# Cutting the token and result transfers of a planned S4-and-MLP kernel in two pieces instead of four, with a newly searched order

## The chip, the cores and the metric

The kernel runs on one core of a Trainium2 chip. The metric is the device time of one execution in microseconds; for the kernel before it is the median of three runs.

## The reference

A token mixer with an S4 convolution and an MLP gate, on 2048 tokens of 512 channels, all float32. Cut to what matters:

```python
xn = layernorm(x)                                  # x = A_u, [1, 2048, 512]
# S4: K[d, l] = Re sum_n C exp(dt A l) dt B, then a long convolution by FFT
y = irfft(rfft(pad(xn)) * rfft(pad(K)))[:L] + xn * Dskip
# MLP on the same xn: two shifted token mixings, then a channel MLP
h = gelu(layernorm(xn) @ w1)
x1 = xn + concat(shift(+1), shift(-1), shift(+2), shift(-2) of h's quarters) @ w2
b = x1 + gelu(layernorm(x1) @ w3) @ w4             # 512 -> 1376 -> 512
return x + y * silu(b)
```

## The kernel before, in words

The tokens lie in one SBUF tile `X` of 128 partitions, 16 slices `s` and 512 channels. Token 64 t + 16 r + s is in partition 32 i + t of slice s, where r is `ORDER[i]` and `ORDER` is 0, 2, 1, 3. A piece of 32 partitions therefore holds one r, and its rows lie 64 tokens apart in memory; within a row the slices are contiguous.

All work is first recorded as operations (matmul, activation, DMA and so on) with what they read and write, by the class `Plan`; nothing is written out in the order in which it runs. `order()` then simulates the engines with a cost for each operation and takes, on each engine, the ready operation with the smallest number in the table `DUE`. The table `PIN` says for each operation that VectorE (DVE) or ScalarE (ACT) could do which of the two does it. Where the simulation sees TensorE (PE) waiting for longer than `LEAST` microseconds it puts idle products (`pick.fill` matmuls of an identity into a spare bank) in front of the waiting matmul. `issue()` writes out ACT's table loads (L496), the idle products (L498) and all operations (L499), so nearly every row of the trace has line 499, and the tile names tell the steps apart. Each engine runs its own list in order. DMAs are issued from SP's list, the result's stores (`E.store`, L630) from SP's or ACT's.

The steps by their tile names:

- `loads()` (L832) brings the S4 parameters (`rawA`, `rawC`), the weights (`w`, `wst`), constants (`ks`, `ev`, `is`), `Dt` (the skip weights, four DMAs of 2 x 64 numbers) and the tokens `X`. The tokens come through `by_r` (L808) for slices 0-1, 2-3, 4-7, 8-11 and 12-15, four DMAs of 32 partitions each time.
- DVE takes `stats` of X slice by slice for the layer norm; DVE or ACT normalise X in place.
- From about 20 to 370 us DVE and ACT build the convolution kernel's phases and magnitudes (`pt`, `mag`), while TensorE transforms the tokens (`uin`, `ue`, `scr_Ud`, `scr_Uh`) and the kernel (`kin`, `k1e`), through scratch tensors in memory.
- The MLP's products `pb<-x1T,w3h` (up) and `pa<-w4h,ghl` (down) fill TensorE's time between the transforms.
- `products` multiplies the spectra (`pr`), `inverse` (L1195) loads `zin` and transforms back, and X is multiplied by the gate in place.
- `finish(g)` (L1215) loads the raw tokens again into `xr`, through `by_r` for four slices at a time, adds them, and stores the result with four DMAs of 32 partitions for each piece of a group.

All DMAs share 8 semaphore lanes in turn; a DMA on a lane waits until the last one on that lane has landed.

Of the kernel before, what the change touches and what calls it, by code (L numbers as in the profile page):

```python
# [24 lines left out]
S = 16  # L25
# [71 lines left out]
class Op:  # L97
# [20 lines left out]
SPAN, LEFT, LEAST = 0.224, 0.3, 0.8  # L118
# [517 lines left out]
def kernel(  # L636
# [579 lines left out]
    xr = {}  # L1216
# [363 lines left out]
```

## Time and profile before

| what | value |
|---|---|
| median of 3 runs | 535.5 us (535.47 to 535.63) |
| the profiled execution | 537.38 us, its span 535.6 us |
| PE, DVE, ACT busy | 511.1, 450.9, 400.8 us |
| bytes moved by the DMA engines | 109.44 MB, mean 204 GB/s |
| granted TensorE clock, mean | 0.99 |

Times inside the execution count from the start of the span. A row of the timeline or of the chain gives start, duration, engine, line, operation, output and inputs, and the number of instructions merged in it. "SPq" and "ACTq" are DMA issues on those engines' queues. A row of a group gives busy time, mean ns of one instruction, and the idle time before it with what ended it. A row of a window gives its length, each engine's busy time with its instructions, the granted clock, the mean busy share of the 16 DMA engines and the rate in GB/s; the share can exceed 1 where packets overlap. A row of a tile gives the shortest, median and longest instruction in ns, with the first and the last start in us. A row of waits gives the sum, the number and the longest.

### The profile page before, as it was taken

How to read it: one execution, taken by the hardware profiler on the slowest of the kernel's cores; microseconds unless marked ns; L12 is line 12 of the kernel's file. 1: busy time of each engine (PE TensorE's matmuls, PEld its weight loads, DVE VectorE, ACT ScalarE, POOL GpSimd, SP SyncE). 2: the span in 40 equal slices, each digit the busy share in tenths (PEclk: the TensorE clock that was granted, in tenths of full speed). 3: DMA queues.
4: the chain of work that ended last, by engine and by line, in shares of the span. 5: the costliest groups of instructions: out<-in, count | busy, mean ns of one | idle time of the engine just before them, and what ended most of it. 6: DMA issues, size and time to landing. Idle time of an engine off the chain costs nothing.

```text
span 535.6 us, 14336 instructions
## 1 busy us (share of the span) xinstructions
PE 511.1 (95%) x6055; PEld 333.1 (62%) x6055; DVE 450.9 (84%) x783; ACT 400.8 (75%) x597; POOL 0.7 (0%) x6
## 2 busy tenths in 40 slices
PE   8789999999999999999999999999999999999992
PEld 8776666774343666565676676666655666566650
DVE  6899999999999999999999999999553267754593
ACT  4999999999998999998989999885336315322420
POOL 0000000000000000000000000000000000000000
PEclk9899999999999999999999999999999999999997
DMA  7994689983886506456333643547989859979986
GB/s 192 258 222 160 227 249 254 281 233 121 296 269 221 101 7 163 140 194 178 112 129 70 180 158 107 118 164 207 251 332 320 282 175 286 258 234 275 310 252 186
DMA packets 95329, 109.44 MB, mean 204 GB/s; under 512 B 40289, under 2 KB 74337, under 8 KB 94369
## 3 DMA queue, kind: packets, MB, share of 16 engines
q1 hardware_dynamic: 94592, 106.95, 69.4%
q10 hardware_dynamic: 672, 1.57, 1.0%
q8 instruction: 47, 0.77, 0.6%
q14 instruction: 18, 0.14, 0.1%
HBM read 64.46 MB, written 37.75 MB: 191 GB/s over the span
## 4 chain that ended last, share of the span: by engine, by line
PE 68%; DVE 10%; ACT 10%; DMA 7%; issue 2%; SPq 2%; ACTq 0%; DVEq 0%
PE pb L499 22%; PE pa L499 22%; PE pd L499 13%; PE pc L499 11%; DVE pt L499 7%; DMA X<-in_A_u_dram 4%; ACT pt L499 3%; SPq L499 2%; ACT ue L499 2%; DVE X L499 1%; ACT L496 1%; DMA scr_Ud<-ue 1%; ACT wst L499 1%; DMA cst<-c_gp 1%; DMA rawC<-in_A_B_re_dram 1%
## 5 line engine op out<-in xcount | busy, mean ns | idle before, releaser
L499 PE MATMUL pb<-x1T,w3h 128*128 128x256 f16 (+1 forms) x1056 | 124.9, 273 | 0.0
L499 PE MATMUL pa<-w4h,ghl 128*128 128x512 f16 (+1 forms) x528 | 123.4, 380 | 0.0
L499 PEld LDWEIGHTS <-w3h 128*128 128x128 f16 (+1 forms) x1056 | 102.6, 100 | 28.8 <-issue 11.6
L499 PEld LDWEIGHTS <-ghl 128*128 128x128 f16 (+1 forms) x528 | 49.4, 98 | 60.6 <-issue 9.2
L499 ACT ACTIVATE g<-pb,wsc 128x512 f32<-128x512 f32 (+1 forms) x48 | 30.7, 650 | 47.6 <-PE pb L499 43.6
L499 ACT ACTIVATE pt<-pt 128x2048 f32<-128x2048 int32 x32 | 61.0, 1908 | 2.4 <-DVE pt L499 2.3
L496 ACT ACT_TABLE_LOAD x48 | 61.6, 1283 | 1.6 <-PEq L1568 0.7
L499 DVE TENSOR_TENSOR pt<-mag,pt 128x1024 f32<-128x1024 f32 x48 | 58.1, 1215 | 0.1
L499 PE MATMUL pd<-w,hT 128*128 128x512 f32 x116 | 53.3, 600 | 2.4 <-DVE X L499 1.9
L499 DVE SCALAR_TENSOR_TENSOR ghl<-g,wsc,ghl 128x512 f16<-128x512 f32 (+1 forms) x48 | 33.5, 700 | 11.6 <-ACT ghl L499 11.3
L499 ACT ACTIVATE mag<-par 128x128 f32<-128x128 f32 x160 | 41.1, 463 | 0.1
L499 ACT ACTIVATE ghl<-g,wsc 128x512 f16<-128x512 f32 (+1 forms) x35 | 24.0, 688 | 20.5 <-PE pa L499 19.0
L499 PEld LDWEIGHTS pd<-w,hT 128*128 128x128 f32 x116 | 21.1, 190 | 27.7 <-issue 23.3
L499 DVE TENSOR_TENSOR pt<-pt 128x2048 f32<-128x2048 f32 x16 | 36.4, 2281 | 0.9 <-ACT pt L499 0.9
L499 PEld LDWEIGHTS pc<-pt 128*32 128x32 f32 x2048 | 29.5, 110 | 8.4 <-issue 5.8
L499 PE MATMUL pc<-pt 128*32 128x64 f32 x2048 | 32.4, 220 | 1.9 <-DVE pt L499 1.0
L499 ACT ACTIVATE pt<-pt,halfpi 128x2048 f32<-128x2048 f32 x16 | 32.0, 1999 | 0.1
L499 PE MATMUL pb<-xT,w 128*128 128x256 f32 x128 | 29.6, 383 | 1.4 <-ACT xT L499 1.4
L499 DVE TENSOR_TENSOR pr<-pd,uin 128x1024 f32<-128x1024 f32 x16 | 19.3, 1219 | 11.5 <-PE pd L499 11.5
L499 PEld LDWEIGHTS pb<-xT,w 128*128 128x128 f32 x128 | 23.6, 190 | 7.8 <-ACT xT L499 3.3
L499 DVE TENSOR_TENSOR pr<-pd,kh 128x1024 f32<-128x1024 f32 x16 | 19.3, 1218 | 6.7 <-PE pd L499 6.0
L499 PE MATMUL pb<-xT,w1h 128*128 128x256 f16 x192 | 22.5, 273 | 0.0
(160 smaller groups left out, 787.8 us busy)
## 6 DMA issues: line engine op xcount, KB each, us to landing
wst<-in_B_w_dram SPq DMA_DIRECT2D x20, 512.0 KB, 5.1
scr_Ud<-ue SPq DMA_DIRECT2D x16, 512.0 KB, 3.9
uin<-scr_Ud SPq DMA_DIRECT2D x32, 256.0 KB, 4.3
cst<-c_gp SPq DMA_DIRECT2D x16, 384.0 KB, 4.0
scr_Uh<-uh SPq DMA_DIRECT2D x8, 512.0 KB, 3.2
scr_Kfa<-k1e SPq DMA_DIRECT2D x8, 512.0 KB, 3.7
kin<-scr_Kfa SPq DMA_DIRECT2D x16, 256.0 KB, 4.1
scr_Zda<-z1e SPq DMA_DIRECT2D x8, 512.0 KB, 5.0
```

The lines of the kernel that those rows point to most:

```text
L496: self.engines["ACT"].preload_act_table_set(SETS[table])
L499: ins = [getattr(self.engines[op.eng], name)(*args, **kw).ins for name, args, kw in op.calls]
```

## The change

- Tokens and result are viewed as `(t b a s) d -> a b t s d`, with a and b of size 2. `by_r` loops over the two a, and each DMA has 64 partitions in SBUF (b and t together) and b of 2 by t of 32 rows in memory. The placement of the tokens in X is the same.
- All stores go through `by_r`, on SP alone. X takes 10 DMAs instead of 20, xr 8 instead of 16, the result 18 instead of 36.
- A wait is filled with idle products for 0.87 of its length (`FILLED`) instead of all of it.
- There are 1796 operations instead of 1832, and `DUE` and `PIN` hold newly searched numbers.

```diff
-SPAN, LEFT, LEAST = 0.224, 0.3, 0.8
+SPAN, LEFT, LEAST, FILLED = 0.224, 0.3, 0.8, 0.87
...
 PIN = (
-    "10111111111111111111111111111111111111111111111110101101101111111100111110010011101111111111101110100000111111"
...
+    "10111111111111111111111111111111111111101001011011111111001111100100111011111111101011101111001111111111100111"
...
-                    pick.fill = max(0, int((t - start - LEFT) / SPAN))
+                    pick.fill = max(0, int((t - start - LEFT) * FILLED / SPAN))
...
-    xv = u[0].rearrange("(t r s) d -> r t s d", r=4, s=S)
-    ov = out[0].rearrange("(t r s) d -> r t s d", r=4, s=S)
+    xv = u[0].rearrange("(t b a s) d -> a b t s d", a=2, b=2, s=S)
+    ov = out[0].rearrange("(t b a s) d -> a b t s d", a=2, b=2, s=S)
...
     def by_r(sb, dr, to_dram=False):
-        for r in range(4):
-            a, d = sb[32 * r : 32 * r + 32], dr[ORDER[r]]
-            Q.dma_start(d, a) if to_dram else Q.dma_start(a, d)
+        for a in range(2):
+            part = sb[64 * a : 64 * a + 64]
+            Q.dma_start(dr[a], part) if to_dram else Q.dma_start(part, dr[a])
...
-        by_r(X[:, 0:2], xv[:, :, 0:2])
+        by_r(X[:, 0:2], xv[:, :, :, 0:2])
...
-            by_r(X[:, s0:s1], xv[:, :, s0:s1])
+            by_r(X[:, s0:s1], xv[:, :, :, s0:s1])
...
-            by_r(xr[q], xv[:, :, 4 * q : 4 * q + 4])
+            by_r(xr[q], xv[:, :, :, 4 * q : 4 * q + 4])
...
-            for r in range(4):
-                E.store(ov[ORDER[r]][:, x], X[32 * r : 32 * r + 32, x])
+            by_r(X[:, x], ov[:, :, :, x], True)
```

SP's list at the start, where the parameters and the first tokens are loaded (shapes are those of the transfer's output side; xN merges equal rows). Before:

```order
L499 DMA rawC<-in_A_C_im_dram 128x2x128
L499 DMA X<-in_A_u_dram 32x1024 x7
L499 DMA ks_81<-c_ks 128x128
L499 DMA X<-in_A_u_dram 32x1024
L499 DMA rawC<-in_A_B_re_dram 128x2x128
L499 DMA wst<-in_B_w_dram 128x4x256
L499 DMA rawC<-in_A_C_re_dram 128x2x128
L499 DMA ev<-c_ev 128x44
L499 DMA rawC<-in_A_B_im_dram 128x2x128
L499 DMA X<-in_A_u_dram 32x2048 x5
```

The same place in the list of the changed kernel:

```order
L497 DMA X<-in_A_u_dram 64x1x1024 x2
L497 DMA rawC<-in_A_C_re_dram 128x2x128
L497 DMA X<-in_A_u_dram 64x1x1024
L497 DMA ev<-c_ev 128x44
L497 DMA X<-in_A_u_dram 64x1x1024
L497 DMA rawC<-in_A_B_re_dram 128x2x128
L497 DMA rawC<-in_A_C_im_dram 128x2x128
L497 DMA X<-in_A_u_dram 64x1x2048
```

Eight pieces of the first four slices became four pieces of 64 partitions; parameters and weights stand between pieces of X as before, `ks` and `wst` later.

SP's list at the end, from the last reloads `xr` to the last store. Before:

```order
L499 DMA xr<-in_A_u_dram 32x2048
L499 DMA zin<-scr_Zdb 128x4x256
L499 DMA xr<-in_A_u_dram 32x2048
L499 DMA zin<-scr_Zdb 128x4x256 x2
L499 DMA zin<-scr_Zda 128x4x256
L499 DMA out_dram<-X 32x1024 x17
L499 DMA out_dram<-X 32x512
L499 DMA out_dram<-X 32x1024
L499 DMA out_dram<-X 32x512 x3
```

The end of SP's list in the changed kernel:

```order
L497 DMA xr<-in_A_u_dram 64x1x2048
L497 DMA scr_Zdb<-z1e 128x1024
L497 DMA xr<-in_A_u_dram 64x1x2048 x5
L497 DMA scr_Zdb<-z1e 128x1024
L497 DMA zin<-scr_Zda 128x4x256 x2
L497 DMA zin<-scr_Zdb 128x4x256 x8
L497 DMA zin<-scr_Zda 128x4x256
L497 DMA out_dram<-X 2x32x1024 x14
L497 DMA out_dram<-X 2x32x512 x4
```

The reloads now stand together in front of eleven loads of `zin`, and all 18 stores follow one another on SP, two for each piece of a group.

ACT's list at its end, with its share of the stores and the gate's last activations (`X<-X`). Before:

```order
L499 ACTIVATE ghl<-g_485,wsc 128x512
L499 ACTIVATE ghl<-g_487,wsc 96x256
L496 ACT_TABLE_LOAD
L499 ACTIVATE warm<-g_487 96x1
L499 DMA out_dram<-X 32x1024 x5
L499 ACTIVATE X<-X 128x512 x2
L499 DMA out_dram<-X 32x1024
L499 DMA out_dram<-X 32x512
L499 DMA out_dram<-X 32x1024
L499 DMA out_dram<-X 32x512 x3
```

The end of ACT's list in the changed kernel:

```order
L497 ACTIVATE ghl<-g_485,wsc 128x512
L497 ACTIVATE g_487<-pb_100,wsc 96x256
L494 ACT_TABLE_LOAD
L497 ACTIVATE warm<-g_487 96x1
L497 ACTIVATE ghl<-g_487,wsc 96x256
L497 ACTIVATE X<-X 128x512 x2
```

No store is left in ACT's list, and the last table load stands ahead of the last `ghl` instead of behind it.

More of the change, by code (lines that the diff above doesn't have):

```diff
@@ L226 @@
 PIN = (
-    "10111111111111111111111111111111111111111111111110101101101111111100111110010011101111111111101110100000111111"
-    "11111001111100100111011111111111110111111111111111111111111111101011011010101111111111111111111111111111111111"
-    "01110110110101011111111111111111111111101111111011011010111111101101101010111111111111111111111111111101111111"
-    "11111111111111111011010111111111110110101111111111111111111111111111110011111110110101010110111101101010111111"
-    "11111111010101010101010101010101111111111111111111111101101111111111111111111111111111111111111111111111111101"
@@ L232 @@
-    "11111111111111111111111111101101111111111111111111111111111111111111111011011111111111111111111101101111101111"
-    "10111110111110111110111110111110111110111110100110011010000000001111110001111111101111111000111111111111111100"
-    "01111111101111111000111111110101000000000111111000111111110111111100011111111011111110001111111101111111000111"
-    "11111011101111110111111001110111001111001111100111101111110011111001111100111001100111100111110011110111111111"
-    "01111001111100111001111111101111110111111101111110111111101111110111111101111110111111101111110111111101111110"
@@ L237 @@
-    "11111110111111011111110111111010100000000011111100011111111011111110001111111101111111000111111110111111100011"
-    "11111111010000000001111110001111111111111111000111111110111111100011111111011111110001111111101110011111001111"
-    "10111110111111110111111001111001111100111110011111001110011001111001111100111100111110011111001111101111011101"
-    "11110111111001111001111100111110111111011110111101111011111100111101111110011111001111100111111100111100111110"
-    "01111001111100111110011111011111100111110011110011011111111011110011100111011111111111110111111111110111111111"
@@ L242 @@
-    "11111111111111011111111111011111111111011111111111111111111111010000000001111111111111111111111111111111111111"
-    "111111111111111100111111011111111110110111111101101011111111001100111100"
+    "10111111111111111111111111111111111111101001011011111111001111100100111011111111101011101111001111111111100111"
+    "11001001110111111111010111111111111111111111111111111010110110101011111111111111111111111111111111110111011011"
+    "01011111111111111111111111111101001110110110101011111011011010101111111111111111111111111011100111111111111111"
@@ new lines @@
+    "11111110110101111111111101101010111111111111111111111111111101110111101101010101101111011010101111111111111101"
+    "01010101010101010101011111111111111111111111011011111111111111111111111111111111111111111111111111011111111111"
+    "11111111111111111011011111111111111111111111111111111111111110110111111111111111111111011011011111111011111011"
+    "11101111101111101111101111101111101001100110100000000011111100011111111011111110001111111111111111000111111110"
+    "11111110001111111101010000000001111110001111111101111111000111111110111111100011111111011111110001111111101110"
@@ new lines @@
+    "11111101111110111100110011110011111001111001111100111110011111001110011001111001111101111101111111110111100111"
+    "11001110011111111011111101111111011111101111111011111101111111011111101111111011111101111111011111101111111011"
+    "11110111111101111110101000000000111111000111111110111111100011111111011111110001111111101111111000111111110101"
+    "00000000011111100011111111011111110001111111101111111000111111111111111100011111111011100111110111111011110011"
+    "10111101111110111110111111011111100111110011101110011110011111001111011111100111110011111011110011011111001111"
@@ L244 @@
+    "10111110011111011111100111110011101111111110011111001111011111100111110011111011111011011111001111100111101111"
+    "11001111101111110111111001111100111100110111111110111101111101111011111111111101111111111111111111111101111111"
+    "11110111111111110111111111110111111111111111111111111100000000011111111111111111111111111111111111111111111111"
+    "111111111111111111111111111111111111"
 )
```

180 rows, old and new, of the table DUE are left out of this document.

## The prediction

> **What bounds the kernel now.** I read the page first: the engines' shares, the queue that carries the data, and the chain of waits.
>
> ```profile
> PE 511.1 (95%) x6055; PEld 333.1 (62%) x6055; DVE 450.9 (84%) x783; ACT 400.8 (75%) x597; POOL 0.7 (0%) x6
> DVE  6899999999999999999999999999553267754593
> q1 hardware_dynamic: 94592, 106.95, 69.4%
> PE 68%; DVE 10%; ACT 10%; DMA 7%; issue 2%; SPq 2%; ACTq 0%; DVEq 0%
> ```
>
> TensorE is busy for 511.1 of 535.6 us, and the chain lies on it for 68%. A change that leaves TensorE's work alone can win only in the rest: the start, a few holes, the end. The queue's line holds a second fact. Its 106.95 MB took 69.4% of 16 engines' 535.6 us, so an engine moved 106.95 MB / (0.694 x 16 x 535.6 us) = 18.0 GB/s while busy. Next I asked for the two ends, in the chain in order of time and in the timeline of SP, ACT and DVE.
>
> ```profile
> 14.20 9.11 DMA X<-in_A_u_dram
> 23.32 10.98 DMA X<-in_A_u_dram
> 517.53 6.60 PE pa L499 x30
> 526.32 1.30 DVE X L499 x2
> ...
> 511.49 21.83 SPq L499 DMA_DIRECT2D out_dram<-X  x22
> 525.60 4.20 ACTq L499 DMA_DIRECT2D out_dram<-X  x6
> 527.65 0.69 DVE L499 TENSOR_TENSOR X<-X,xr 128x512 f32<-128x512 f32 x1
> SPq L499 <- DMA out_dram<-X: 9.9, 5, 5.4
> ```
>
> At the head the chain runs for 20 us over loads of X. At the tail TensorE stops at 524.13, the last residual add at 527.65 + 0.69 = 528.34, and SP issues stores until 511.49 + 21.83 = 533.32: the span ends 7.3 us after the last add. SP spends 9.9 us of that stretch on other stores' landings, 5.4 at once. What the change touches are thus X's loads, the reloads xr, and the stores, and how long each takes sets both ends.
>
> **The change part by part.** First the bytes, from the page's list of transfers:
>
> ```profile
> X<-in_A_u_dram SPq DMA_DIRECT2D x12, 256.0 KB, 8.5
> X<-in_A_u_dram SPq DMA_DIRECT2D x8, 128.0 KB, 3.9
> xr<-in_A_u_dram SPq DMA_DIRECT2D x16, 256.0 KB, 5.3
> out_dram<-X SPq DMA_DIRECT2D x18, 128.0 KB, 2.1
> out_dram<-X ACTq DMA_DIRECT2D x10, 128.0 KB, 3.2
> out_dram<-X ACTq DMA_DIRECT2D x4, 64.0 KB, 2.0
> out_dram<-X SPq DMA_DIRECT2D x4, 64.0 KB, 1.7
> ```
>
> X is 4.19 MB, xr 4.19 and the result 4.19. All three are recut by one edit, and not only in number: a piece was 32 rows against 32 rows. Now its SBUF side is 64 partitions, and its memory side is `b` = 2 outermost, then `t` = 32. The two sides share only one outermost cut, the one in halves. If a transfer is dealt to the engines by its outermost dimension, as I take it to be, a piece of 32 went to 16 engines and a piece of 2 x 32 goes to 2.
>
> The nearest rows to such a pattern are Dt's loads, the only ones before with 2 outermost:
>
> ```profile
> L499 SPq DMA_DIRECT2D Dt<-in_A_Dskip_dram x4: 579/593/770, 21.0 to 35.4; - x4
> L499 SPq DMA_DIRECT2D X<-in_A_u_dram x20: 311/419/472, 5.9 to 34.3; - x20
> L499 DVE BATCH_NORM_STATS2 stats<-X x16: 658/682/694, 11.9 to 49.7; 128x6 f32<-128x512 f32 x16
> L499 SPq DMA_DIRECT2D xr<-in_A_u_dram x16: 310/420/1523, 372.4 to 501.8; - x16
> 372.39 2.85 SPq L499 DMA_DIRECT2D xr<-in_A_u_dram  x4
> 478.93 1.74 SPq L499 DMA_DIRECT2D xr<-in_A_u_dram  x4
> 509.55 0.36 SPq L499 DMA_DIRECT2D zin<-scr_Zda  x1
> DMA to landing us min/median/max: 3.0/6.9/11.0
> ```
>
> (The last of these lines is for the loads of X.) They show the price on SP: 0.59 us an issue against 0.42 (X, 20 issues to 10, so 8.4 us of SP's time to 5.9; nobody waits for that difference). They don't show engines: Dt's 0.5 KB prints no landing time. In the trace's semaphore records, which no view prints, each of them has fewer updates than a piece of X; that speaks for the dealing, on a transfer too small to have a price.
>
> The Trainium skill, "DMA: Bandwidth & Descriptors", section on why a DMA increments its semaphore by 16, states such a rule: the number of engines is the largest one up to 16 that divides the slowest dimension of size over 1 on both sides, and the hardware queues take the lowest-numbered engines. By it all three transfers go over engines 0 and 1, as in my sum; without it, evenly spread, the sum is rival B's. No run so far shows it for a large transfer.
>
> What two engines are worth is in the windows:
>
> ```profile
> 0.00:12.00 12.00, 10.65 (x73) 10.65 (x74) 7.74 (x24) 5.31 (x14) 0.70 (x6) 1.00 0.75 191
> 12.00:40.00 28.00, 22.71 (x153) 20.05 (x151) 26.09 (x100) 27.46 (x73) 0.00 (x0) 0.94 1.05 239
> 390.00:395.00 5.00, 5.00 (x48) 2.97 (x34) 3.95 (x5) 1.23 (x2) 0.00 (x0) 1.00 1.02 413
> 480.00:490.00 10.00, 10.00 (x118) 7.03 (x116) 5.51 (x8) 2.68 (x4) 0.00 (x0) 1.00 1.00 264
> 490.00:500.00 10.00, 10.00 (x92) 6.05 (x91) 3.89 (x6) 6.44 (x7) 0.00 (x0) 1.00 1.01 299
> 500.00:512.00 12.00, 12.00 (x186) 7.08 (x185) 7.42 (x11) 2.10 (x3) 0.00 (x0) 1.00 1.09 298
> ```
>
> An engine in full use moved 413 / (16 x 1.02) = 25.3 GB/s at best, and 239 / (16 x 1.05) = 14.2 at worst, when sixteen competed. Two that run nearly alone compete with little, so I take 25.3; 18.0 and 14.2 stay for the range.
>
> *Head.* 191 x 12 + 239 x 28 = 9.0 MB move in the first 40 us, of which 4.8 are not X. Engine 0 now carries 4.8/16 = 0.30 and X's half, 2.10: 2.40 MB, 95 us at 25.3. From about 2 us on, X is complete at 97; before, DVE's last statistics of X ran at 49.7 to 50.4. DVE executes in order, and the page has it at 9 tenths or more from its third slice (27 us) on, so little can be made up: +47 us (+85 at 18.0, +121 at 14.2). Transfers issued behind X wait too, since each has a sixteenth of its bytes on those engines; within these 47 us they are counted already.
>
> *Reload at 372 us.* xr's first quarter, 1.05 MB, occupies the two engines for 0.52 / 25.3 = 21 us, in front of spectra that TensorE reads soon after. Between nothing and 21: 10.
>
> *Tail.* Three quarters of xr (1.57 MB an engine) are issued from about 479 on, as before. The last three windows carry 9.2 MB from 480 to 512, less 3.15 of xr 6.1, a sixteenth 0.38. Then 2.10 of stores: 1.95 / 25.3 = 77 us, 2.10 / 25.3 = 83 us, and some 5 between them until the first result is ready (0 to 10). 479 + 77 + 5 + 83 = 644, and with 47 and 10 the span ends at 701. Nothing hides this: TensorE's remaining work after 479 is 45 us.
>
> *Stores on SP alone.* 36 issues on two queues become 18 on one. The 5.4 us hole (a store on SP waits for one of ACT's queue, which stands behind the last silu) goes. Spread over 16 engines, the end would be the last add, 528.34, two issues of 0.6, and a landing of 2.1: 531.6 against 535.6, **-4.0**. On two engines nothing of that is seen, since the drain decides.
>
> *Idle products and the new order.*
>
> ```profile
> L496 ACT ACT_TABLE_LOAD x48 | 61.6, 1283 | 1.6 <-PEq L1568 0.7
> 79.24 1.60 PE L498 MATMUL pd<-ident 128*128 128x128 f32 x12
> 111.44 0.83 PE L498 MATMUL pa<-ident 128*128 128x128 f32 x6
> 465.39 5.70 DMA cst<-c_gp
> ```
>
> The order has 4 table loads less (at most 4 x 1.283 = 5.1 us, on an engine that waits elsewhere), and 51 idle products for 57, none of them past the first 40 us; the two late groups, 1.60 and 0.83, stand in waits that stay. The chain's wait for cst may go. I put these at **-2** together, between -5.1 and +2.4 (if the two late groups' waits prove longer in the new order). In the two-engine case this drowns.
>
> **The sum.** The profiled execution took 537.38 us, its span 535.6, 1.8 around it; the median of the runs, 535.5, is 1.9 less. Forecast: 701 + 1.8 - 1.9 - 2 + 2 for the last landing, **701 us**. Its own range: if only half of the head's delay passes on, and neither 10 nor 5 is paid, 479 + 77 + 83 + 24 = 663, and 660 with the order's gain; a little faster engine leads to 650. At 18.0 GB/s: 479 + 108 + 117 + 5 + 85 + 15 = 809, which I think too slow for engines that compete with little, so 790.
>
> **The rivals.**
>
> *B, faster: the transfers still go over 16 engines*, because the queue cuts them by rows or bytes and not by the outermost dimension. For it: every large transfer of before runs that way, and the windows with a share above 1.00 show all sixteen filled. Against it: none of those has 2 outermost, and Dt's records. Then SP's queue at the end decides: 537.38 - 4.0 - 2 - 1.9 = **529.5**, between 526 and 534 (-5.1 and +2.4 in the place of -2). Chance 0.14.
>
> *C: one side alone decides.* If only the side read counts, X and xr go over 2 engines and the stores over 16: 479 + 77 + 47 + 10 = 613, then the last 15 us of TensorE's work from its last zin load (509) to 524 and the 7.5 of the end: 636. If the side written counts, only the stores do: first store 511.5 before, 83 us of drain: 595, less what the order gains. **585 to 645**, chance 0.06.
>
> **How the numbers follow.** A (two engines) has 0.80: the pattern allows nothing else if dealing goes by the outermost dimension, and the one row of this kind has records that fit. A's own range, 650 to 790, holds it 19 times in 20, 0.76 of all; with most of C, down to 600, 0.80. B is left out. Of this kernel a measurement can tell 0.2%, 1.1 us. Slower by more: A and C, 0.86. Of B 0.13 is faster by more, 0.01 within.
>
> **What would show it.** If A holds: the windows after 12 us show a DMA share far below 0.3 while X loads, the statistics of X end near 97 us and not 50, X's landings take tens of us where they took 3.0 to 11.0, and after TensorE's end stores drain for over 80 us at about 2 x 25 = 50 GB/s. If B holds: statistics end before 50 us, TensorE ends at 521 to 526, the span about 7.5 us after it, and SP's wait for stores in front of its last issues is gone. C shows one end like A's, the other like B's. A is wrong if landings of X stay near 10 us; its rate is wrong if the drain runs at 28 or 36 GB/s, and its term for the head if statistics end late but TensorE's end moves by less.

## The result and the profile after

The changed kernel takes 728.17 us (median of 4 runs, 727.12 to 729.13) against 535.57: a ratio of 1.3585, with a 95% interval of 1.3551 to 1.3619. It is slower by 193 us, the two-engine case A, 27 us above its number. The lines of its page that answer to those of before:

```profile
PE 527.1 (73%) x6043; PEld 342.3 (47%) x6043; DVE 455.3 (63%) x787; ACT 393.2 (54%) x589; POOL 0.7 (0%) x6
PE   7234667998999999999999997499999910290000
PEclk9586786999999999999999999699999965595555
q1 hardware_dynamic: 94184, 108.52, 51.4%
PE 53%; SPq 12%; DMA 11%; ACT 6%; DVE 6%; issue 1%; DVEq 0%
```

The engines' work is the same to within some us, apart from 16 more on TensorE. The span is 191 us longer, and the zeros and low digits of the PE row say where: at the start (slices 2 to 7), for a moment in the middle, in slices 33 to 35, and at the end, where nothing computes in the last 4 slices. In the chain of waits SP's queue has risen from 2% to 12% and DMA from 7% to 11%.

The windows of the changed kernel at those places (length, engines' busy time, granted clock, DMA share, GB/s):

```profile
20.00:50.00 30.00, 10.79 (x65) 10.24 (x66) 8.32 (x31) 5.18 (x21) 0.00 (x0) 0.64 0.30 90
50.00:100.00 50.00, 29.86 (x129) 23.02 (x128) 21.09 (x82) 23.41 (x51) 0.00 (x0) 0.76 0.33 105
445.00:460.00 15.00, 4.00 (x25) 2.19 (x23) 1.24 (x2) 0.69 (x1) 0.00 (x0) 0.70 0.13 51
657.00:726.00 69.00, 0.00 (x0) 0.00 (x0) 0.03 (x1) 0.00 (x0) 0.00 (x0) 0.50 0.13 52
```

A share of 0.13 is that of two engines of sixteen, 0.125, always busy. The trace's packet records, which no view prints, bear this out: for 94% of the time from 660 to 720 us exactly two packets are under way. They move 51 and 52 GB/s, 26 each. That holds for reads (xr at 445) and for writes (stores at 657) alike, so it is neither the side read alone nor the side written alone that decides, and rival C falls here already. In both directions it is the memory side that has the 2; whether the SBUF side counts too is not shown, since it has 32 or 64 partitions in every run here.

Who waits, in the changed kernel (waiter, what it waits for, sum, times, longest), and the tiles' rows behind it:

```profile
24.97 0.69 DVE L497 BATCH_NORM_STATS2 stats<-X 128x6 f32<-128x512 f32 x1 [13.81 <-DMA X<-in_A_u_dram]
DVE stats L497 <- DMA X<-in_A_u_dram: 55.1, 5, 15.2
PE pd L497 <- DMA cst<-c_gp: 15.6, 1, 15.6
PE pc L497 <- DMA zin<-scr_Zda: 46.1, 1, 46.1
104.89 0.69 DVE L497 BATCH_NORM_STATS2 stats<-X 128x6 f32<-128x512 f32 x1 [15.17 <-DMA X<-in_A_u_dram]
109.23 0.69 DVE L497 BATCH_NORM_STATS2 stats<-X 128x6 f32<-128x512 f32 x1
652.74 1.09 PE L497 MATMUL pc<-zin,is 64*32 64x256 f32 x32
656.34 0.69 DVE L497 TENSOR_TENSOR X<-X,xr 128x512 f32<-128x512 f32 x1
```

Only the first wait is for a transfer that was recut. `cst` and `zin` have their old form; they stand behind xr in SP's list. SP's own rows in the timeline, and one row of the chain, show what holds them:

```profile
7.25 5.82 SPq L497 DMA_DIRECT2D ev<-c_ev  x1
437.58 21.26 SPq L497 DMA_TRANSPOSE x1T<-x1s  x1
558.79 0.57 SPq L497 DMA_DIRECT2D xr<-in_A_u_dram  x1
560.82 31.27 SPq L497 DMA_DIRECT2D xr<-in_A_u_dram  x5
592.18 9.42 SPq L497 DMA_DIRECT2D scr_Zdb<-z1e  x1
601.71 29.07 DMA zin<-scr_Zda
638.72 76.03 SPq L497 DMA_DIRECT2D out_dram<-X  x18
```

Single issues that took 0.3 to 0.6 us, and a transpose that takes 1.2 to 2.7 in the run with 16 rows further down, take 5 to 21 here: SP stands in the issue itself. That it waits for room behind the two loaded engines fits, but no row shows how full a queue is. The wait for `cst` is SP's: the load was issued at 459.57, after the 21 us, and its products went on at 464.55. The wait for `zin` began at 584.7, so 17 of its 46 us passed before the issue at 601.71; the chain gives the load itself 29.07. Its share on the two loaded engines stands behind xr there, if it is dealt over all sixteen.

Two rows of the tile `pr` serve as milestones, of before and then of the changed kernel (shortest, median and longest in ns, first and last start in us):

```profile
L499 PE MATMUL pd<-pr,cst x128: 376/376/480, 269.3 to 395.9; 64*128 64x256 f32 x128
L499 DVE TENSOR_TENSOR pr<-pd,uin x16: 1214/1217/1225, 434.3 to 483.3; 128x1024 f32<-128x1024 f32 x16
```

```profile
L497 PE MATMUL pd<-pr,cst x128: 376/376/480, 334.1 to 477.9; 64*128 64x256 f32 x128
L497 DVE TENSOR_TENSOR pr<-pd,uin x16: 1214/1218/1225, 515.1 to 563.7; 128x1024 f32<-128x1024 f32 x16
```

The times add up: first spectra product `pd<-pr,cst` +65; first `pr<-pd,uin` +81; last residual add's end 528.3 and 657.0, +129; span 535.6 and 726.6, +191. So the head cost 65, the reload in the middle 16, the wait for zin 48, the drain of the stores 62. (This compares two orders; against the order of the changed kernel without the loss, the table further down has 62.6, 17.3, 48.5 and 65.3.)

### The profile page after: what moved, and what is told of

Same layout as the page of the kernel before. It is cut to its first block, busy times and chain, and to the rows that moved or that the text cites. A ratio compares the mean times of both kernels' runs of the same rounds, so it can differ in the third digit from the quotient of the medians.

```text
span 726.6 us, 14248 instructions
## 1 busy us (share of the span) xinstructions
PE 527.1 (73%) x6043; PEld 342.3 (47%) x6043; DVE 455.3 (63%) x787; ACT 393.2 (54%) x589; POOL 0.7 (0%) x6
## 4 chain that ended last, share of the span: by engine, by line
PE 53%; SPq 12%; DMA 11%; ACT 6%; DVE 6%; issue 1%; DVEq 0%
PE pb L497 19%; PE pa L497 16%; SPq L497 12%; PE pd L497 10%; PE pc L497 9%; DVE pt L497 4%; DMA X<-in_A_u_dram 4%; DMA zin<-scr_Zda 4%; DMA w<-in_B_w_dram 3%; ACT mag L497 2%; ACT pt L497 2%; ACT L494 1%; DMA cst<-c_gp 1%; DVE X L497 1%; ACT uh L497 0%
## 5 line engine op out<-in xcount | busy, mean ns | idle before, releaser
L497 PE MATMUL pb<-x1T,w3h 128*128 128x256 f16 (+1 forms) x1056 | 126.9, 276 | 0.0
L497 DVE BATCH_NORM_STATS2 stats<-X 128x6 f32<-128x512 f32 x32 | 21.6, 684 | 55.1 <-DMA X<-in_A_u_dram 55.1
L497 PE MATMUL pc<-zin,is 64*32 64x256 f32 x144 | 6.5, 436 | 46.1 <-DMA zin<-scr_Zda 46.1
L497 PE MATMUL pc<-pt 128*32 128x64 f32 x2048 | 34.1, 225 | 3.5 <-DVE pt L497 2.6
L497 DVE TENSOR_TENSOR X<-X,pc 128x512 f32<-128x512 f32 x9 | 6.2, 685 | 47.4 <-PE pc L497 47.3
L497 PEld LDWEIGHTS pc<-pt 128*32 128x32 f32 x2048 | 31.1, 113 | 9.8 <-issue 4.6
L497 PE MATMUL pb<-xT,w 128*128 128x256 f32 x128 | 32.1, 404 | 3.8 <-DMA w<-in_B_w_dram 3.8
```

Of the source, the lines that this page charges most:

```text
L497: ins = [getattr(self.engines[op.eng], name)(*args, **kw).ins for name, args, kw in op.calls]
```

## The experiments

D is the theory of the prediction's case A: a transfer is dealt to as many engines as the outermost dimension has cuts. P: pieces of 64 partitions are slow by themselves. O: the new order and the idle products cost the time. A ratio compares a run with the kernel before in the same session, where its median was 536.63 us, in the last experiment 537.2; so gains are read from the ratios and not against 535.5.

**Sixteen outermost rows.** With b = 16 the memory side of a piece is 16 x 4 rows; the same 64 partitions, bytes and queue, and an order equal row for row.

```diff
-    xv = u[0].rearrange("(t b a s) d -> a b t s d", a=2, b=2, s=S)
-    ov = out[0].rearrange("(t b a s) d -> a b t s d", a=2, b=2, s=S)
+    xv = u[0].rearrange("(t b a s) d -> a b t s d", a=2, b=16, s=S)
+    rv = u[0].rearrange("(t b a s) d -> a b t s d", a=2, b=16, s=S)
+    ov = out[0].rearrange("(t b a s) d -> a b t s d", a=2, b=16, s=S)
...
-            by_r(xr[q], xv[:, :, :, 4 * q : 4 * q + 4])
+            by_r(xr[q], rv[:, :, :, 4 * q : 4 * q + 4])
```

> The changed kernel with one number altered: the memory side of every piece of X, xr and the result has 16 outermost by 4 rows in place of 2 by 32. Pieces, bytes, issue form, queue and order stay the same; the tokens come to lie in other partitions, so the numbers computed are other ones. Theory D (a transfer is dealt to as many engines as the outermost dimension has cuts, two in the changed kernel): the statistics of X end before 55 us, stores drain in under 12 us after TensorE's end, 526 to 534 us in all. Rival P (pieces of 64 partitions whose two sides have different dimensions are slow by themselves): within 2% of 728. Rival O (the new order and the idle products cost the time): over 600.

534.45 us, half a microsecond above D's range, a ratio of 0.9959 to before (0.9945 to 0.9973). One number in the views takes back all of the 193 us. P and O are out as causes of the loss. The tail's rows of this run:

```profile
span 532.9 us, 14248 instructions
527.94 0.69 DVE L497 TENSOR_TENSOR X<-X,xr 128x512 f32<-128x512 f32 x1
510.30 19.83 SPq L497 DMA_DIRECT2D out_dram<-X  x18
SPq L497 <- DVE X L497: 7.9, 5, 2.4
```

The span ends 4.3 us after the last add, where it was 7.3 before and 70 in the changed kernel. SP now waits for DVE's adds and no longer for other stores.

**Four pieces in the new order.** Each step of `by_r` issues two pieces of 32 partitions.

```diff
         for a in range(2):
-            part = sb[64 * a : 64 * a + 64]
-            Q.dma_start(dr[a], part) if to_dram else Q.dma_start(part, dr[a])
+            with plan.together(cost=ISSUE):
+                for b in range(2):
+                    part = sb[64 * a + 32 * b : 64 * a + 32 * b + 32]
+                    pair = (dr[a][b], part) if to_dram else (part, dr[a][b])
+                    Q.dma_start(*pair)
+                    plan.group.dma += dma_cost(pair)
```

(The rest of the edit lets whatever uses a place next wait for both pieces.)

> The changed kernel with each transfer of X, xr and the result issued as two pieces of 32 partitions again, both in one step of the plan, so that the new order, the idle products and the stores on SP stay. D: 16 engines again, 527 to 533 us, the gain over 535.5 from the tail (TensorE's end to the span's end about 8 us and not 11.5) and some 2 us of the order. P: the same, so this run tells D and P apart from O only. O: over 600. If the tail gains nothing with 36 issues on one queue: 533 to 536.

534.23 us, 0.9955 (0.994 to 0.9969), 1.2 us above D's 533. It beats before by 0.45%, as the run above does by 0.41%: the number of pieces and of issues makes no difference that can be told between the two. It moves the same rows into the same partitions as the changed kernel, so the addresses and the placement don't cost the time either; only the cut into transfers differs.

**Before, with all stores on SP.**

```diff
-                E.store(ov[ORDER[r]][:, x], X[32 * r : 32 * r + 32, x])
+                Q.dma_start(ov[ORDER[r]][:, x], X[32 * r : 32 * r + 32, x])
```

> The kernel before with one line altered: all 36 stores on SP, none on ACT, everything else as it was. If the tail's term was right (a store on SP waits for one that stands behind the last silu in ACT's list): the span ends 3 to 4 us earlier, 531.5 to 533 us. Rival: 36 issues at 0.37 us on one queue take the place of the wait, 535 to 537.

535.14 us, 0.9978 (0.9967 to 0.999): 1.2 us won, a third of what was expected, and a time in the rival's range. The tail of this run:

```profile
526.91 0.69 DVE L499 TENSOR_TENSOR X<-X,xr 128x512 f32<-128x512 f32 x1
510.75 20.43 SPq L499 DMA_DIRECT2D out_dram<-X  x36
SPq L499 <- DVE X L499: 7.4, 5, 4.9
```

The wait for another store is gone from the top of the list, and SP is held by DVE's add instead, 4.9 us at once. From the last add (end 527.60) to the span's end, 533.5, are 5.9 us. Of 7.3 only 1.4 are won, since SP's issues go on until 531.18.

**Before, with waits filled to 0.87.**

```diff
-SPAN, LEFT, LEAST = 0.224, 0.3, 0.8
+SPAN, LEFT, LEAST, FILLED = 0.224, 0.3, 0.8, 0.87
...
-                    pick.fill = max(0, int((t - start - LEFT) / SPAN))
+                    pick.fill = max(0, int((t - start - LEFT) * FILLED / SPAN))
```

> The kernel before with waits filled to 0.87 by idle products, everything else as it was. My term for it was nothing by itself: 535 to 536 us. Rival: idle products that end late delay the work behind them, then 0.5 to 2 us are won; or the clock granted to TensorE falls in the first 40 us, then it loses 0.5 to 2.

536.22 us, 0.9993 (0.9984 to 1.0003): nothing that can be told.

**Eight and four outermost rows.** As the first experiment, with b = 8 and b = 4.

> As the run with 16 outermost, but 8 outermost by 8 rows (other tokens in the partitions again). D: eight engines at 25 GB/s, 200 GB/s for these transfers: X at the head takes 4.19 MB / 200 = 21 us and is nearly hidden, the tail's drain grows little; 530 to 550 us. P: 728.

> The same with 4 outermost by 16 rows. D: four engines: the engine's load in each stretch is half of the changed kernel's. Head: 1.05 + 0.30 MB at 25.3 is 53 us, so X complete at 58 to 65 and the head late by 15 to 25; the tail 0.79 + 0.38 + 1.05 MB is 88 us after 479, with about 10 before the first store; 585 to 625 us. P: 728.

567.39 and 612.44 us, a single run each. The time falls with every step from 2 outermost to 16: 728, 612, 567, 534. The losses against 16 are 194, 78 and 33 us. If the load of an engine counts, they go as 1/k - 1/16, that is 0.438, 0.188 and 0.063: 443, 416 and 528 us for one unit. Two and four lie near one line, eight a fifth to a quarter above it. Taken apart by the milestones used above, against the run with 16 (us):

| outermost | head | reload | wait for zin | end | in all |
|---|---|---|---|---|---|
| 2 | 62.6 | 17.3 | 48.5 | 65.3 | 193.7 |
| 4 | 24.4 | 9.8 | 18.5 | 25.1 | 77.8 |
| 8 | 14.3 | 1.6 | 11.9 | 4.9 | 32.7 |

Four was as expected. Eight was not: with a range up to 550 about 16 us were allowed, and X was to be nearly hidden. The head alone lost 14, and the wait for zin, for which nothing had been put in, 12. The head's windows in the run with eight, two of the run with 16 and one of that with 4:

```profile
20.00:35.00 15.00, 10.02 (x74) 9.81 (x72) 9.83 (x48) 8.20 (x32) 0.00 (x0) 0.84 0.80 166
35.00:50.00 15.00, 13.18 (x66) 11.90 (x66) 10.83 (x38) 12.47 (x32) 0.00 (x0) 0.81 0.74 173
...
5.00:20.00 15.00, 13.47 (x109) 12.80 (x108) 12.25 (x41) 11.02 (x27) 0.00 (x0) 1.00 1.04 243
20.00:35.00 15.00, 10.92 (x82) 9.87 (x83) 14.79 (x58) 14.94 (x50) 0.00 (x0) 1.00 1.05 277
...
20.00:35.00 15.00, 11.05 (x74) 10.70 (x74) 6.70 (x28) 4.96 (x21) 0.00 (x0) 0.76 0.55 156
```

With eight a busy engine moved 166 / (16 x 0.80) = 13.0 GB/s and 14.6, with sixteen 14.6 and 16.5, with four 17.7, and not the 25.3 that I had put in for eight. It is not the number of engines that lowers the rate. The head of the changed kernel, with two, gives 90 / (16 x 0.30) = 18.8 by the same working, which averages over all engines that were busy, the loaded two among them; and where the stores drain with nothing beside them, four engines and eight move as much each as two:

```profile
582.00:600.00 18.00, 0.00 (x0) 0.00 (x0) 0.00 (x0) 0.00 (x0) 0.00 (x0) 0.50 0.26 106
557.00:563.00 6.00, 0.00 (x0) 0.00 (x0) 0.00 (x0) 0.00 (x0) 0.00 (x0) 0.50 0.51 203
```

These are 106 / (16 x 0.26) = 25.5 GB/s with four and 203 / (16 x 0.51) = 24.9 with eight. The low rates belong to the head, where other loads run beside X; what makes them low there is not shown. The shares of 0.26 and 0.51 are four and eight engines of sixteen, and the packet records agree: in these stretches four packets are under way for 86% of the time, and eight for 70%. So do the records of completions: with 16, 8, 4 and 2 outermost a trace has 4764, 4506, 4368 and 4295 of them. For each of the 36 pieces that is about four fewer from 8 to 4 and two fewer from 4 to 2, one for an engine.

**One of the three transfers in two.** 2 outermost for one, 16 for the other two. In these three runs, as in those with 16, 8 and 4, tokens lie in other partitions. Where X, xr and the result are cut differently, the rows that are added or stored no longer belong together, so these three serve for their times alone.

```diff
     xv = u[0].rearrange("(t b a s) d -> a b t s d", a=2, b=2, s=S)
-    ov = out[0].rearrange("(t b a s) d -> a b t s d", a=2, b=2, s=S)
+    rv = u[0].rearrange("(t b a s) d -> a b t s d", a=2, b=16, s=S)
+    ov = out[0].rearrange("(t b a s) d -> a b t s d", a=2, b=16, s=S)
...
-            by_r(xr[q], xv[:, :, :, 4 * q : 4 * q + 4])
+            by_r(xr[q], rv[:, :, :, 4 * q : 4 * q + 4])
```

(This is X alone; for the others the 2 stands in `ov` or `rv`.)

> 2 outermost for X's loads alone, 16 outermost for xr and the stores. D: the head alone, about 65 us later than with 16 engines everywhere: 588 to 602 us. If the head's delay were partly made up in the middle: 560 to 585.

> 2 outermost for the stores alone, 16 outermost for X and xr. D: 2.10 MB at 26 GB/s an engine from the first store on: first store about 512 us minus the order's gain, plus 80: 585 to 600 us. A rule by the side that is read (64 partitions here) would give 530.

> 2 outermost for the reloads xr alone, 16 outermost for X and the stores. D, if the terms add up: X alone brought 63 us over the run with 16 everywhere and the stores alone 63, so of the 194 that the changed kernel lost against it 68 are left for xr: about 16 for the first quarter (a wait of TensorE for cst) and 46 to 52 for the wait for zin before the last groups; 595 to 605 us. If they overlap with the others: under 585.

597.28, 597.84 and 597.16 us, a single run each: 62.8, 63.4 and 62.7 above the 534.45 with 16 everywhere. The sum, 188.9, is the loss of the changed kernel against that run, 193.7, to within 5. Each run shows its own wait, and of the waits of the other two none above 0.7 us:

```profile
DVE stats L497 <- DMA X<-in_A_u_dram: 46.2, 4, 14.6
...
PE pd L497 <- DMA cst<-c_gp: 14.5, 1, 14.5
PE pc L497 <- DMA zin<-scr_Zda: 45.0, 1, 45.0
...
528.00:590.00 62.00, 0.00 (x0) 0.00 (x0) 0.33 (x1) 0.00 (x0) 0.00 (x0) 0.50 0.13 52
```

In the order of these rows: X alone, with its statistics; xr alone, with cst and zin; the stores alone, with 62 us in which two engines drain. So the head's delay isn't made up anywhere, and nothing is hidden twice. The stores alone, read from 64 partitions, lose as much as X alone, so a rule by the side read is out.

**Pieces of 32 partitions with 2 outermost.** The version with four pieces, with a view whose memory side is 2 x 16 rows.

```diff
-    xv = u[0].rearrange("(t b a s) d -> a b t s d", a=2, b=2, s=S)
-    ov = out[0].rearrange("(t b a s) d -> a b t s d", a=2, b=2, s=S)
+    xv = u[0].rearrange("(t c b a s) d -> a b c t s d", a=2, b=2, c=2, s=S)
+    ov = out[0].rearrange("(t c b a s) d -> a b c t s d", a=2, b=2, c=2, s=S)
```

> Pieces of 32 partitions, as many as in the kernel before, with 2 outermost by 16 rows on the memory side, for X, xr and the result (other tokens in the partitions). D: the load of the two engines is the changed kernel's, 715 to 745 us. Rival P (the size of a piece in partitions does it): 534.

719.62 us, a single run. Pieces of 32, as many as in the kernel before, lose nearly as much. With the first experiment this crosses both: size of the piece without effect, outermost dimension with all of it.

**The new order, wholly filled.** The version with four pieces, `FILLED` = 1.0.

> The version with pieces of 32 in the new order, with waits filled wholly by idle products and not to 0.87. As in the kernel before, the factor is worth nothing that can be told: 533 to 535 us. If the new order needs it, 1 to 2 us more.

536.49 us, 0.9981 (0.9967 to 0.9995), where 0.87 gave 0.9955 (0.994 to 0.9969). The two intervals still touch, and the runs were made in different sessions on different chips, so 0.87 may be worth about 1.4 us in the new order; it isn't settled, and what would carry it wasn't looked into.

## Why the prediction was right, and where its sizes were off

- *Two engines.* Right. Two of sixteen at 26 GB/s, reading and writing, the packets under way and the dose from 2 to 16 show it. The Trainium skill's rule ("DMA: Bandwidth & Descriptors", why a DMA increments its semaphore by 16) stands behind it: the runs with 2, 4, 8 and 16 outermost agree. That the engines are the lowest-numbered isn't shown by a view here.
- *The head, +47.* Too small by 13 to 16: the last statistics of X came 59.5 us later, and X alone cost 62.8. Two steps of its sum were short. X was complete at 104.9 and not at 97: the first piece was issued at 4.9, where the sum began at 2, and the sum's own 2.40 MB, an estimate, over the 100 us from there are 24.0 GB/s and not 25.3. And the sum took X's completion for the end of its statistics: five more had to follow, to 109.9. That is 8 and 5 us.
- *Reload in the middle, 10 of 0 to 21.* 15.6 measured on cst, 16 by the milestones. The way to it was only in part the one that the prediction named: SP stood for 21 us in an issue behind xr, and `cst` was issued after that.
- *Start of the tail.* Head and reload together came to 80 (xr's issue at 558.8, before 478.9) and not 57. This is 23 of the 26 us by which the span's 701 was short.
- *The tail, 77 + 5 + 83 = 165.* 558.8 to 726.6 is 168. Right in both terms: the first store was issued 79.9 us after xr (638.72), where 77 + 5 stood, and from there to the end are 87.9, where 83 stood.
- *Stores on SP, -4.0 with 16 engines.* -3.0 in the run with 16 rows, -2.6 with four pieces, -1.4 in the kernel before, each from the last add to the span's end. I had 1.2 of issues and a landing of 2.1 behind the last add. With 16 rows there are 4.3 us: a store of the new form lands in 3.6 (the row is of the run with 16 rows, KB and median us to landing), and SP isn't free at once.

```profile
out_dram<-X SPq DMA_DIRECT2D x14, 256.0 KB, 3.6
```

- *The order and the fill, -2.* About nothing, or a loss: the runs with 16 rows and with four pieces won 2.2 and 2.4 us by their ratios, less than the 3.0 and 2.6 of their ends. In single traces the last add ends at 528.63 and 526.38, before at 528.34. So rival B's own number, 529.5, was too good: what it describes measures 0.9959 x 535.5 = 533.3.
- *Rival C.* Out: the side read alone, or the side written alone, would have left one end as it was.
- *The signs named for A.* They fit less well than the sum. While X loads the share is 0.30 and 0.33, not far below 0.3, since other loads run beside it. The drain after TensorE's end, at 653.8, takes 73 us at 52 GB/s, not over 80 at 50. X's landings are not printed; its first two pieces, issued from 4.86 on, were awaited until 24.97.

## What to carry to other kernels

Before a DMA is recut, look at the outermost dimension as the transfer will carry it, here that of the memory side; fewer, larger pieces are no gain if the outermost count falls from 32 to 2. A share of 2/16 at 52 GB/s while all engines are idle is how it looks in a profile (0.30 where other loads run beside it), and the transfers that are seen waiting may be others in the same queue. Here pieces of 16 x 4 rows lost nothing against twice as many of 32, so the outermost dimension can be chosen by the view, if the tokens' placement may follow it.

## What the runs showed of the hardware that was not expected

Draining stores alone, a DMA engine moved 25 to 26 GB/s whether two, four or eight were loaded. In the head, beside other loads, a busy one moved 18.8 with two, 17.7 with four, 13.0 to 14.6 with eight and 14.6 to 16.5 with sixteen. A rate taken from one stretch of a kernel doesn't carry over to another.

SP's issue isn't of constant length: with two loaded engines behind it, the issue of `ev`, 0.58 us in the run with 16 rows, took 5.82, and a transpose, at most 2.65 there, 21.26, so a loaded queue holds back every transfer in SP's list, of whatever form. The granted clock of TensorE fell to 0.50 in stretches in which it was idle, and to 0.64 in the head (0.862 over the span, 0.99 before); TensorE's busy time is 16 us longer at the same work. The run with 16 rows issues the same products in the same order in 510.5 us at a clock of 0.99, so the order is not the reason; the lower clock fits, though no run separated it.
